# Rebuilding the attention part of a fused cross-read and expert-router kernel

## The chip, the cores and the metric

The kernel runs on one core of one Trainium2 chip. The metric is the device time of one execution in microseconds (us). Engines are written as in the profile: PE is TensorE (PEld its weight loads), DVE is VectorE, ACT is ScalarE, POOL is GpSimd, and SP issues most of the transfers.

## The reference, cut to what matters

Two parts follow each other. The first part has 8 batches of 8 heads; each head has 512 rows `x` and 32 states, both 64 wide. The second part sends each of the 8 x 544 resulting rows of 512 features to one of 8 experts.

```python
# first part, per batch and head (B, H, S, Ns, D = 8, 8, 512, 32, 64)
a  = softmax(scale * x @ state.T)      # over the 32 states of a row
xread = a @ state
a2 = softmax(scale * state @ x.T)      # over the 512 rows of a state
sread = a2 @ x
rows = concatenate([xread, sread])     # (512 + 32) rows of a batch; heads side by side: 512 features
# second part (N, D, E, F = 4352, 512, 8, 1024)
logits = normalize(rows) @ normalize(expert_emb).T / tau
e = argmax(logits);  gate = softmax(logits)[e]
out = gate * (relu(rows @ w1[e]) @ w2[e])
```

Everything is computed in fp32. The scores `x @ state.T` and `state @ x.T` of the first part are the same numbers, transposed.

## The kernel before

The program has three stages: the **attention part**, a **seam** that sorts the rows into blocks of one expert, and the **second part**, a loop over 41 blocks of 128 rows. The change lies in the attention part alone; the two other stages have the same instructions before and after.

A **unit** is one batch and one group of 4 heads, so that there are 16 units; 4 heads with 32 states each make 128 state rows, and 4 heads with 64 features make 256 columns. The states of a group stand as a block diagonal of 128 x 256 (`bdst`, with the 8 projections on the experts behind it, width 264).

- `states(b)`, once a batch: POOL copies the states into the block diagonal (L184), PE transposes it (`st_ps`, L190), ACT copies it out as `bd`, and PE projects it on the experts (`pj_ps`, L198).
- `scores(b, g)`: PE transposes the rows (`xt_ps`, L214, eight transposes), DVE and ACT copy a half each out as `xT`. PE then computes the scores twice: `sT_ps` with the states in partitions (L218) and `s_ps` with the rows in partitions (L223). The softmax over rows works on `sT_ps` and ends in `e2` and a diagonal matrix `dg` of the reciprocals of the sums (L238). The softmax over states works on `s_ps` and ends in `e1`, by the chain of a maximum (L245), a subtraction (L246), the exponential on ACT (L247), a sum (L248), a reciprocal (L250) and a multiplication on POOL (L251).
- `reads(b, g)`: PE transposes `e1` (`a_ps`, L258), turns `e2` by a matmul with `dg` that also scales it (`e_ps`, L263), and computes the two reads, `x_ps` (L270) and `sr_ps` (L278). The four `x_ps` banks are copied out by DVE and ACT in turns.
- `rows(b)` stores a batch's rows and chooses experts (`choose`); `state_rows(g)` does so for the state rows of 4 batches, after batches 3 and 7.

In the loop over units `scores` of unit u+1 is written ahead of `reads` of unit u, so it runs one unit ahead. A scheduler places each engine's instructions in one order that is fixed when the program is built; an engine then takes them strictly in that order, and a wait holds everything behind it. Most tiles of the loop (xn, xT, e1, e2 and others) have two buffers, PSUM has eight banks in rotation. A transfer takes one of eight semaphores in turn, and waits until the transfer that had it before has landed. `load_x` brings a batch's rows in four transfers, `load_w1` one expert's first weights.

Of the kernel before, what the change touches and what calls it, by code (L numbers as in the profile page):

```python
# [19 lines left out]
def kernel(  # L20
# [75 lines left out]
    with ExitStack() as att_ctx:  # L96
        att1 = att_ctx.enter_context(tc.tile_pool(name="att1", bufs=1))
        att = att_ctx.enter_context(tc.tile_pool(name="att", bufs=2))

# [10 lines left out]
        st_nat = att1.tile([P, B, HG, Dh], FP32, name="st_nat")  # L110
        nc.sync.dma_start(
            st_nat.rearrange("p b g d -> p (b g) d"),
            state.rearrange("b (g i) n d -> (i n) (b g) d", g=HG),
        )
# [458 lines left out]
```

## Time and profile before

| what | value |
|---|---|
| time, three runs | 885.47, 887.55 and 893.33 us (median 887.55) |
| the profiled execution, span from first to last instruction | 891.5 us (the profile lists no other time of it) |
| attention part, to the end of the last `sr_ps` matmuls | 0 to 209.1 us |
| seam, to the first transposes of a gathered block | 209.1 to 256.3 us |
| second part | 256.3 to 891.5 us |
| busy share of the span | PE 93%, PEld 52%, DVE 26%, ACT 16%, POOL 14% |

The span lies between the second and the third of the runs, 0.4% above the median. In the profile, "busy" of PE includes modelled ends of pipelined matmuls. Each fp32 matmul that is not a transpose shows as two instructions (two `sT_ps` matmuls as x4), a transpose as one. "PEclk" is the granted share of TensorE's full clock.

### The profile page before, as it was taken

The page shows a single profiled execution, that of the slowest core. Times are in us where ns is not written, and L with a number is a line of the kernel's source. Part 1 is how long each engine was busy: PE and PEld are TensorE (multiplying, and loading weights), DVE is VectorE, ACT ScalarE, POOL GpSimd, SP SyncE. Part 2 cuts the span into 40 slices and gives each one's busy share as a digit, 9 for nine tenths or more (in the row PEclk, how much of TensorE's full clock was granted, in tenths as well). Part 3 has the DMA queues.
Part 4 walks back from the last instruction along what each step waited for, and adds up shares of the span by engine and source line. Part 5 has one row for each costly group of instructions (what it writes and reads, how often), then busy time and mean ns, then how long its engine had stood idle before and what let it go on. Part 6 is the DMA issues. An engine that isn't in the chain of part 4 may idle for free.

```text
span 891.5 us, 8858 instructions
## 1 busy us (share of the span) xinstructions
PE 830.0 (93%) x3280; PEld 467.8 (52%) x3280; DVE 234.2 (26%) x514; ACT 138.5 (16%) x280; POOL 125.0 (14%) x192
## 2 busy tenths in 40 slices
PE   6899999995659999999999999999999999999995
PEld 4677777774624444454545454444444454545442
DVE  3454556546211112121212121211111121212110
ACT  3343444443001000000000010101000000000000
POOL 2111111110120111111111111111111111110000
PEclk9899999997569999999999999999999999999998
DMA  9486844311073454555545464636464545545340
GB/s 269 156 285 189 260 130 95 72 49 60 0 248 103 144 195 159 176 178 161 193 149 198 136 207 132 215 132 219 134 204 145 186 168 171 174 154 188 123 163 0
DMA packets 97553, 140.84 MB, mean 158 GB/s; under 512 B 38174, under 2 KB 46366, under 8 KB 97512
## 3 DMA queue, kind: packets, MB, share of 16 engines
q1 hardware_dynamic: 90920, 120.59, 41.9%
q0 software_dynamic: 6560, 19.67, 6.6%
q8 instruction: 27, 0.44, 0.2%
q14 instruction: 14, 0.11, 0.0%
q10 hardware_dynamic: 32, 0.02, 0.0%
HBM read 122.44 MB, written 19.66 MB: 159 GB/s over the span
## 4 chain that ended last, share of the span: by engine, by line
issue 62%; PE 20%; POOL 10%; DVE 5%; DMA 2%; POOLq 1%; ACT 1%; DVEq 0%
PE sT_ps L218 5%; POOL out_dram L517 4%; POOL xin L462 4%; PE s_ps L223 3%; PE x_ps L270 3%; PE sr_ps L278 3%; PE inv_ps L427 2%; PE e_ps L263 1%; DVE xT L70 1%; PE pj_ps L198 1%; DMA xin<-x_rows,src_row 1%; PE a_ps L258 1%; DMA x_rows<-xs 1%; PE xt_ps L214 1%; PE st_ps L190 1%
## 5 line engine op out<-in xcount | busy, mean ns | idle before, releaser
L512 PE MATMUL y_ps<-w,hT 128*128 128x512 f32 x656 | 292.4, 599 | 0.6 <-ACT hT L68 0.6
L486 PE MATMUL h_ps<-w_sb,xT 128*128 x656 | 289.4, 594 | 0.0
L486 PEld LDWEIGHTS h_ps<-w_sb,xT 128*128 128x128 f32 x656 | 125.1, 191 | 157.3 <-issue 157.2
L512 PEld LDWEIGHTS y_ps<-w,hT 128*128 128x128 f32 x656 | 121.3, 190 | 142.2 <-issue 137.3
L494 ACT ACTIVATE h<-h_ps 128x512 f32<-128x512 f32 x41 | 24.5, 597 | 467.6 <-PE h_ps L486 467.6
L516 DVE TENSOR_SCALAR y<-y_ps,gpos 128x512 f32<-128x512 f32 x41 | 30.8, 751 | 250.6 <-PE y_ps L512 250.6
L496 DVE TENSOR_SCALAR h<-h_ps 128x512 f32<-128x512 f32 x41 | 28.4, 692 | 254.4 <-PE h_ps L486 254.4
L517 POOL DMA_INDIRECT out_dram<-y,dst_row x41 | 41.6, 1015 | 307.5 <-DVE y L516 307.5
L462 POOL DMA_INDIRECT xin<-x_rows,src_row x41 | 42.2, 1030 | 261.0 <-PE xt_ps L475 237.8
L505 PEld LDWEIGHTS ht_ps<-ident,h 128*128 128x128 f32 x328 | 38.3, 140 | 21.6 <-issue 21.6
L218 PE MATMUL sT_ps<-xT,bd 128*128 128x512 f32 x64 | 40.9, 772 | 7.4 <-DVE xT L70 7.2
L68 ACT ACTIVATE hT<-ht_ps 128x512 f32<-128x512 f32 x41 | 24.5, 597 | 138.6 <-PE ht_ps L505 138.6
L505 PE MATMUL ht_ps<-ident,h 128*128 128x128 f32 x328 | 42.5, 272 | 0.0
L223 PEld LDWEIGHTS s_ps<-bd,xT 128*128 128x128 f32 x256 | 33.1, 200 | 11.1 <-issue 11.1
L475 PE MATMUL xt_ps<-ident,xin 128*128 128x128 f32 x164 | 25.6, 280 | 9.9 <-DMA xin<-x_rows,src_row 9.9
L270 PE MATMUL x_ps<-bdst,aT 128*128 128x264 f32 x128 | 33.4, 405 | 0.0
L278 PEld LDWEIGHTS sr_ps<-xn,a 128*32 128x32 f32 x512 | 29.0, 110 | 5.5 <-DVE r L248 4.5
L278 PE MATMUL sr_ps<-xn,a 128*32 128x64 f32 x512 | 31.6, 220 | 0.0
L223 PE MATMUL s_ps<-bd,xT 128*128 128x64 f32 x256 | 31.4, 277 | 0.0
L477 DVE COPY xT<-xt_ps 128x512 f32<-128x512 f32 x41 | 27.9, 681 | 10.6 <-PE xt_ps L475 10.6
L70 DVE COPY hT<-ht_ps 128x512 f32<-128x512 f32 x41 | 28.4, 692 | 7.6 <-PE ht_ps L505 6.9
L427 PE MATMUL inv_ps<-rr,oh 128*128 128x82 f32 x68 | 14.8, 422 | 15.5 <-POOL rr L420 15.5
(127 smaller groups left out, 469.4 us busy)
## 6 DMA issues: line engine op xcount, KB each, us to landing
w<-in_moe_w_dram SPq DMA_DIRECT2D x41, 2048.0 KB, 10.1
w_sb<-in_moe_w_dram SPq DMA_DIRECT2D x8, 2048.0 KB, 9.7
xn<-in_x_dram SPq DMA_DIRECT2D x32, 256.0 KB, 4.8
x_rows<-xr SPq DMA_DIRECT2D x16, 512.0 KB, 4.4
xin<-x_rows,src_row POOLq DMA_INDIRECT x41, 3.7
out_dram<-y,dst_row POOLq DMA_INDIRECT x41, 7.8
st_nat<-in_state_dram SPq DMA_DIRECT2D x1, 512.0 KB, 4.7
x_rows<-xs SPq DMA_DIRECT2D x2, 256.0 KB
```

The costliest lines, as they stand in the source:

```text
L70: eng.tensor_copy(dst, src)
L218: nc.tensor.matmul(sT, lhsT=bd[:, g, j], rhs=xT[:, j], start=(j == 0), stop=(j == 1))
L223: nc.tensor.matmul(s[:, c * P + j * half : c * P + j * half + half], lhsT=xT[:, j, c * P : c * P + P], rhs=bd[:, g, j, j * half : j * half ...
L270: nc.tensor.matmul(ps[:, 0:XW], lhsT=aT[:, c * P : c * P + P], rhs=bs[:, g], start=True, stop=True)
L278: nc.tensor.matmul(ps[q0 : q0 + Ns, i * Dh : i * Dh + Dh], lhsT=a2[:, c * P + i * Ns : c * P + i * Ns + Ns], rhs=xn[:, c, (HPG * g + i) * ...
L427: nc.tensor.matmul(inv_ps[:, 0 : 2 * NBLK], lhsT=oh[:, s], rhs=rr[:, s].rearrange("p t k -> p (t k)"), start=(s == 0), stop=(s == NSLOT - 1),)
L462: nc.gpsimd.indirect_dma_start(out=t, out_offset=None, in_=x_rows[:], in_offset=bass.IndirectOffsetOnAxis(ap=src_row[:, j : j + 1], axis=0 ...
L486: nc.tensor.matmul(ps, lhsT=xT[:, k * P : k * P + P], rhs=w1f[:, ds(ek * (KD * F) + k * F + i * 512, 512)], start=(k == 0), stop=(k == KD ...
L505: nc.tensor.transpose(ps[:, k * P : k * P + P], h[:, f0 : f0 + P], ident)
L512: nc.tensor.matmul(ps, lhsT=hT[:, k * P : k * P + P], rhs=w2[:, k], start=(k == 0), stop=(k == KF - 1))
L516: nc.vector.tensor_scalar(y, ps, gpos[:, j : j + 1], None, ALU.mult)
L517: ins = nc.gpsimd.indirect_dma_start(out=out[:], out_offset=bass.IndirectOffsetOnAxis(ap=dst_row[:, j : j + 1], axis=0), in_=y, in_offset= ...
```

## The change

The attention part gets a new shape.

- **Scores once.** Only `sT_ps` is computed, each pair of heads as a matmul of its own with 64 state columns, into a half of the partitions (L281 of the changed kernel). `s_ps` is gone. `e1` is now made by DVE's transpose of 32 x 32 squares from `sT_ps` (L295); the subtraction moves from DVE to POOL (L298); after the multiplication on POOL (L306) a second DVE transpose makes `aT` directly (L308). `a_ps` and its copy are gone.
- **State weights scaled, then transposed.** ACT multiplies `e2` by the reciprocal sums (L302); `e_ps` is now four transposes (L315) and no matmul with `dg`. ACT copies `e_ps` out (L317), and all four `x_ps` banks (L323); DVE no longer does.
- **States prepared once.** All transposed states (`bd`) and projections (`proj`) are made before the first unit, from two copies of the states in other layouts that come by ten transfers on ACT's queue, ahead of `emb` and `tau`. `states(b)` is then four transfers of 256-byte pieces into the block diagonal and a POOL copy of 8 columns a group.
- **Two units ahead.** `turn` of unit u+2 stands ahead of `reads(u)`, `scores` of u+2 behind it. `xT` halves, `aT` and `e2` have three buffers. The batches' rows come three batches ahead; every third batch lies in the place of the last expert's `w1`, whose load waits for that.

The core of the diff (comments that were removed are left out):

```diff
...
+        spare = w1_sb[:, E - 1].rearrange("p k f -> p (k f)")
         def load_x(b):
-            t = att.tile([P, NCH, D], FP32, tag="xn", name="xn")
+            if b % 3 == 2:
+                t = spare[:, 0 : NCH * D].rearrange("p (c d) -> p c d", c=NCH)
+            else:
+                t = att.tile([P, NCH, D], FP32, tag="xn", name="xn")
...
+        for b in range(B):
+            p0 = Ns * (b % 4)
+            nc.scalar.dma_start(st_row[p0 : p0 + Ns, b // 4], state[b].rearrange("h n d -> n h d"))
+        st_nat = [att.tile([P, B, Dh], FP32, tag="e2", name="st_nat", bufs=3) for _ in range(HG)]
+        for g in range(HG):
+            nc.scalar.dma_start(
+                st_nat[g], state[:, HPG * g : HPG * g + HPG].rearrange("b i n d -> (i n) b d")
+            )
...
         def states(b):
             bs = bdst[b % 2]
             for i in range(HPG):
-                nc.gpsimd.tensor_copy(
-                    bs[Ns * i : Ns * i + Ns, :, Dh * i : Dh * i + Dh], st_nat[Ns * i : Ns * i + Ns, b]
-                )
...
+                nc.sync.dma_start(
+                    bs[Ns * i : Ns * i + Ns, :, Dh * i : Dh * i + Dh],
+                    state[b].rearrange("(g i) n d -> i n g d", g=HG)[i],
+                )
+            nc.gpsimd.tensor_copy(bs[:, :, GW:XW], proj[:, b])
+            return bs
...
             sT = bank("sT_ps")
             for j in range(2):
-                nc.tensor.matmul(sT, lhsT=bd[:, g, j], rhs=xT[:, j], start=(j == 0), stop=(j == 1))
-            s = bank("s_ps")
...
+                o = j * 2 * Ns
+                nc.tensor.matmul(
+                    sT[o : o + 2 * Ns], lhsT=bd[b // 4][:, b % 4, 2 * g + j], rhs=xT[j], start=True, stop=True
+                )
...
+            nc.vector.transpose(e1f, sT)
             nc.scalar.activation(e2, sT, AF.Exp, bias=r2[:, 0:1], scale=SCALE, accum_out=r2[:, 1:2])
+            nc.vector.tensor_reduce(r1[:, 0].unsqueeze(2), e1, axis=AX, op=ALU.max)
+            nc.gpsimd.tensor_tensor(e1, e1, bc(r1[:, 0], shp, 2), ALU.subtract)
+            nc.scalar.activation(e1, e1, AF.Exp, scale=SCALE)
...
+            nc.scalar.activation(e2, e2, AF.Copy, scale=r2[:, 2:3])
...
             nc.gpsimd.tensor_tensor(e1, e1, bc(r1[:, 1], shp, 2), ALU.mult)
+            aT = att.tile([P, S], FP32, tag="aT", name="aT", bufs=3)
+            nc.vector.transpose(aT, e1f)
+            return aT, e2
...
             for c in range(NCH):
-                nc.tensor.matmul(
-                    ps[:, c * P : c * P + P], lhsT=e2[:, c * P : c * P + P], rhs=dg, start=True, stop=True
-                )
+                nc.tensor.transpose(ps[:, c * P : c * P + P], e2[:, c * P : c * P + P], ident)
...
-            if u + 1 < len(units):
-                b1, g1 = units[u + 1]
-                ready[u + 1] = scores(b1, g1, x_nat[b1], st[b1][1])
-            reads(b, g, x_nat[b], st[b][0], xr[b], *ready.pop(u))
+            later = u + 2 < len(units)
+            if later:
+                b2, g2 = units[u + 2]
+                xT = turn(b2, g2, x_nat[b2])
+            reads(b, g, x_nat[b], st[b], xr[b], *ready.pop(u))
+            if later:
+                ready[u + 2] = scores(b2, g2, xT)
```

The order of PE in one unit of the steady part, before (unit 1: the rows up to `s_ps` are unit 2's scores, with batch 1's states ahead of them):

```order
L190 MATMUL st_ps<-ident,bdst_107 128x128 x4
L198 MATMUL pj_ps<-enT,bd 128x8 x4
L214 MATMUL xt_ps<-ident,xn 128x128 x8
L218 MATMUL sT_ps<-xT,bd 128x512 x2
L223 MATMUL s_ps<-bd,xT 128x64 x8
L258 MATMUL a_ps<-ident,e_249 128x128 x4
L263 MATMUL e_ps<-dg,e_240 128x128 x4
L270 MATMUL x_ps<-bdst_106,aT 128x264 x4
L278 MATMUL sr_ps<-xn,a_373 32x64 x16
```

And in the changed kernel (unit 4; `sT_ps` at the end is unit 6's):

```order
L272 MATMUL xt_ps<-ident,xn 128x128 x8
L315 MATMUL e_ps<-ident,e_547 128x128 x4
L320 MATMUL x_ps<-bdst_121,aT 128x264 x4
L328 MATMUL sr_ps<-w_sb,a_690 32x64 x16
L281 MATMUL sT_ps<-xT,w_sb 64x512 x2
```

`st_ps`, `pj_ps`, `s_ps` and `a_ps` have left the loop, and `sT_ps` of the unit after next stands last.

The order of PE ahead of the first unit's reads in the changed kernel (`en_ps` are the experts, L151 and L159; `sb_ps` and `pj_ps` make the projections; two units' scores follow):

```order
L151 MATMUL en_ps<-ident,begin 128x8 x4
L159 MATMUL en_ps<-ident,begin 128x8 x8
L217 MATMUL st_ps<-ident,begin 128x128 x8
L234 MATMUL sb_ps<-ident,st_nat 128x128 x8
L242 MATMUL pj_ps<-begin 128x64 x8
L272 MATMUL xt_ps<-ident,xn 128x128 x8
L281 MATMUL sT_ps<-xT,w_sb 64x512 x2
L272 MATMUL xt_ps<-ident,xn 128x128 x8
L281 MATMUL sT_ps<-xT,w_sb 64x512 x2
L272 MATMUL xt_ps<-ident,xn 128x128 x8
L315 MATMUL e_ps<-ident,e_249 128x128 x4
L320 MATMUL x_ps<-bdst_121,aT 128x264 x4
```

Before, `en_ps` x4, `st_ps` x4 and `pj_ps` x4 stood ahead of the first `xt_ps`; now 12, 16 and 8 such steps do, and all of them stand behind the experts' row, the first on PE.

The order of DVE before in one unit (here `r2_343`, `r1_352` and `e1_353` belong to unit 2, `a2_373` to unit 1):

```order
L233 TENSOR_REDUCE r2_343<-sT_ps_331 128x1
L234 TENSOR_SCALAR r2_343<-r2_343 128x1
L245 TENSOR_REDUCE r1_352<-s_ps_334 128x16
L236 TENSOR_SCALAR r2_343<-r2_343 128x1
L246 TENSOR_TENSOR e1_353<-s_ps_334,r1_352 128x512
L237 RECIPROCAL r2_343<-r2_343 128x1
L267 COPY a2_373<-e_ps_368 128x512
L238 TENSOR_SCALAR dg_345<-ident_61,r2_343 128x128
L248 TENSOR_REDUCE r1_352<-e1_353 128x16
```

And in the changed kernel, around unit 6 (`r2_799`, `e1_804` and `sT_ps_796` belong to unit 7; `e1_730`, `r1_729` and `aT_743` to unit 6):

```order
L287 TENSOR_REDUCE r2_799<-sT_ps_796 128x1
L303 TENSOR_REDUCE r1_729<-e1_730 128x16
L288 TENSOR_SCALAR r2_799<-r2_799 128x1
L295 STREAM_TRANSPOSE e1_804<-sT_ps_796 128x512
L304 TENSOR_SCALAR r1_729<-r1_729 128x16
L344 TENSOR_TENSOR lg_70<-xr_670 128x32
L297 TENSOR_REDUCE r1_803<-e1_804 128x16
L305 RECIPROCAL r1_729<-r1_729 128x16
L201 TENSOR_REDUCE lmax_71<-lg_70 128x4
L70 COPY xT_849<-xt_ps_851 128x512
```

Before, a unit's own chain stands together up to its sum. Now unit 6's last transpose, `aT_743` (L308), stands three rows further on, and unit 7's maximum, the first of these rows, stands ahead of unit 6's sum (L303), reciprocal (L305) and last transpose, so those wait until `sT_ps` of unit 7 is there.

## Rows read from the trace of the kernel before

**Rows 1.** The page: its first line

```profile
span 891.5 us, 8858 instructions
```

**Rows 2.** Stretches: us, busy (instructions) of PE, PEld, DVE, ACT, POOL, clock, DMA share, GB/s

```profile
24.84:209.06 184.22, 171.13 (x1321) 136.46 (x1321) 95.72 (x277) 75.67 (x177) 28.60 (x68) 0.94 0.49 148
256.33:891.50 635.17, 624.92 (x1804) 303.15 (x1804) 112.19 (x164) 48.98 (x82) 80.58 (x79) 0.99 0.49 163
```

**Rows 3.** Timeline of PE over one unit and the next states: start, us, operation [idle before]

```profile
45.82 1.09 PE L214 MATMUL xt_ps<-ident,xn 128*128 128x128 f32 x8
47.54 1.98 PE L218 MATMUL sT_ps<-xT,bd 128*128 128x512 f32 x4 [0.62 <-DVE xT L70]
49.36 1.89 PE L223 MATMUL s_ps<-bd,xT 128*128 128x64 f32 x16
51.09 0.61 PE L258 MATMUL a_ps<-ident,e 128*128 128x128 f32 x4
51.54 1.06 PE L263 MATMUL e_ps<-dg,e 128*128 128x128 f32 x8
52.43 2.00 PE L270 MATMUL x_ps<-bdst,aT 128*128 128x264 f32 x8
54.37 1.97 PE L278 MATMUL sr_ps<-xn,a 128*32 128x64 f32 x32
56.27 0.66 PE L190 MATMUL st_ps<-ident,bdst 128*128 128x128 f32 x4
...
58.53 1.07 PE L214 MATMUL xt_ps<-ident,xn 128*128 128x128 f32 x8
```

**Rows 4.** Groups of instructions from 40 to 210 us: shapes, count | busy us, mean ns

```profile
L297 ACT ACTIVATE junk<-xr 128x512 f32<-128x512 f32 x32 | 20.1, 627 | 0.6
...
L251 POOL TENSOR_TENSOR e<-e,r 128x512 f32<-128x512 f32 x14 | 14.7, 1048 | 60.5 <-DVE r L250 60.0
...
L68 ACT ACTIVATE xr<-x_ps 128x264 f32<-128x264 f32 x30 | 11.7, 390 | 9.5 <-PE x_ps L270 8.1
...
L235 ACT ACTIVATE e<-sT_ps,r 128x512 f32<-128x512 f32 x14 | 9.6, 688 | 40.6 <-DVE r L234 40.6
...
L260 ACT ACTIVATE aT<-a_ps 128x512 f32<-128x512 f32 x15 | 9.0, 598 | 10.6 <-PE a_ps L258 10.6
...
L70 DVE COPY xT<-xt_ps 128x512 f32<-128x512 f32 x13 | 8.9, 688 | 3.0 <-PE xt_ps L214 2.9
...
L250 DVE RECIPROCAL r<-r 128x16 f32<-128x16 f32 x14 | 3.4, 242 | 0.0
...
L237 DVE RECIPROCAL r<-r 128x1 f32<-128x1 f32 x14 | 2.1, 153 | 0.0
```

**Rows 5.** Timeline of PE: one of the five slow `sT_ps` groups

```profile
83.31 3.58 PE L218 MATMUL sT_ps<-xT,bd 128*128 128x512 f32 x4 [0.68 <-DVE xT L70]
```

**Rows 6.** Stretches, columns as in rows 2: the start, and one slow `sT_ps` group

```profile
2.00:14.00 12.00, 6.84 (x26) 5.30 (x27) 2.69 (x11) 5.42 (x8) 4.62 (x28) 1.00 1.26 223
84.00:88.00 4.00, 4.00 (x15) 2.33 (x14) 0.84 (x2) 0.16 (x1) 0.00 (x0) 0.63 0.72 291
```

**Rows 7.** Timeline of the start, of PE and of ACT's transfer queue

```profile
0.76 0.62 ACTq L117 DMA_DIRECT2D emb<-in_moe_expert_emb_dram  x1
...
3.02 0.63 ACT L130 ACTIVATE junk<-emb 8x512 f32<-8x512 f32 x1
...
6.33 0.56 PE L138 MATMUL en_ps<-ident,emb 8*128 8x8 f32 x4 [6.33 <-POOL bdst L184]
6.82 1.15 PE L190 MATMUL st_ps<-ident,bdst 128*128 128x128 f32 x4
...
12.48 3.36 PE L218 MATMUL sT_ps<-xT,bd 128*128 128x512 f32 x4
...
26.86 2.98 PE L270 MATMUL x_ps<-bdst,aT 128*128 128x264 f32 x8
```

**Rows 8.** Timeline of PE: `state_rows` in the middle of the attention part

```profile
118.50 1.06 PE L314 MATMUL lg_ps<-enT,xsT 128*128 128x8 f32 x8 [0.95 <-DVE xsT L311]
```

More of the change, by code (lines that the diff above doesn't have):

```diff
@@ L108, in load_w1 @@
             nc.sync.dma_start(w1_sb[:, e], moe_w1[e].rearrange("(k p) f -> p k f", p=P))
[L110 to L113, printed above, removed]
-        )
+        begin = [att.tile([P, NCH * HG * XW], FP32, tag="xr", name="begin") for _ in range(2)]
+        st_row = begin[0][:, 0 : 2 * D].rearrange("p (q h d) -> p q h d", q=B // 4, h=H)
+        for b in range(B):
[6 more added lines that the diff above has]
+            )
         x_nat = {0: load_x(0)}
-        emb = att1.tile([P, D], FP32, tag="xsT", name="emb")[0:E]
+        emb = begin[1][0:E, 2 * D : 3 * D]
         nc.scalar.dma_start(emb, moe_expert_emb[:])
@@ L178, in choose @@
                 nc.gpsimd.tensor_tensor(cumx[:, s + 1], cumx[:, s], eq[:, s], ALU.add)
+        nbd = 4 * (H // 2) * 2 * Ns
+        bd = [spare[:, NCH * D : NCH * D + nbd], att1.tile([P, nbd], FP32, name="bd")]
+        bd = [t.rearrange("p (b j n) -> p b j n", b=4, j=H // 2) for t in bd]
+        for q in range(B // 4):
+            nc.vector.memset(bd[q], 0.0)
+            ps = bank("st_ps")
+            for j in range(H // 2):
+                nc.tensor.transpose(
+                    ps[:, j * P : j * P + P],
+                    st_row[:, q, 2 * j : 2 * j + 2].rearrange("p h d -> p (h d)"), ident,
+                )
+            src = ps.rearrange("p (j b n) -> p b j n", b=4, n=Ns)
+            for o in range(2):
+                copy(
+                    (nc.vector, nc.scalar)[o],
+                    bd[q][o * Dh : o * Dh + Dh, :, :, o * Ns : o * Ns + Ns],
+                    src[o * Dh : o * Dh + Dh],
+                )
+        sTb = begin[0][:, 2 * D : 4 * D].rearrange("p (g q n) -> p g q n", g=HG, q=B // 2)
+        for g in range(HG):
+            ps = bank("sb_ps")
+            for q in range(B // 2):
+                nc.tensor.transpose(
+                    ps[:, q * P : q * P + P], st_nat[g][:, 2 * q : 2 * q + 2].rearrange("p b d -> p (b d)"), ident
+                )
+            copy((nc.vector, nc.scalar)[g], sTb[:, g].rearrange("p q n -> p (q n)"), ps)
+        proj = att1.tile([P, B, HG, E], FP32, name="proj")
+        pp = bank("pj_ps").rearrange("p (g q c) -> p g q c", g=HG, q=B // 2)
+        for g in range(HG):
+            for q in range(B // 2):
+                nc.tensor.matmul(
+                    pp[:, g, q], lhsT=sTb[:, g, q], rhs=enb[:, g].rearrange("p b i e -> p (b i e)"),
+                    start=True, stop=True,
+                )
+        for i in range(HPG):
+            for g in range(HG):
+                copy(
+                    (nc.vector, nc.scalar)[g],
+                    proj[Ns * i : Ns * i + Ns, :, g].rearrange("p (q b) e -> p q b e", b=2),
+                    pp[Ns * i : Ns * i + Ns, g].rearrange("p q (b i e) -> p q b i e", b=2, e=E)[:, :, :, i],
+                )
         def states(b):
@@ L221, in scores @@
[L221 to L228 removed]
+                o = j * 2 * Ns
+                nc.tensor.matmul(
+                    sT[o : o + 2 * Ns], lhsT=bd[b // 4][:, b % 4, 2 * g + j], rhs=xT[j], start=True, stop=True
+                )
```

96 lines of the change are left out of this document (37 added, 59 removed).

## The prediction, on record before the changed kernel was timed

> **What bounds the kernel now.** I read the page first, for the span [rows 1], then the stretches [rows 2], then PE's timeline over one unit [rows 3]. The second part, 635.2 us with PE busy for 98% of it, has the same instructions afterwards, and so has the seam; I let both stand. What can move is the attention part, which ends at 209.1 us. From the first unit's reads on, at 24.84 us, PE is busy for 171.1 of 184.2 us (93%), while DVE has 95.7, ACT 75.7 and POOL 28.6 us [rows 2]. In the timeline one group of matmuls follows the other, and the one idle place in the unit shown is 0.62 us ahead of `sT_ps` [rows 3]. So PE's own work bounds this stage; the other engines have slack, but a change that takes work from PE soon meets their chains.
>
> [...]
>
> **PE's work in a unit.** Start to start in the timeline, a unit has `xt_ps` 1.1 (without its wait), `sT_ps` 1.82, `s_ps` 1.73, `a_ps` 0.45, `e_ps` 0.89, `x_ps` 1.94 and `sr_ps` 1.90 us; half of the units have 2.26 us for states besides [rows 3]. The change takes away `s_ps` (1.73), `a_ps` (0.45), half of `e_ps` (four transposes, like `a_ps`: 0.45 for 0.89) and the states (1.13 a unit). What is left is 1.1 + 0.45 + 1.94 + 1.90 + 1.82 = 7.2 us, for 11.0 plus the waits: some 60 us over 16 units, if nothing else took PE's place.
>
> **The other engines' work in a unit.** ACT, by the mean durations [rows 4]: `xT` and `e_ps` copies 2 x 0.6, two exponentials of 0.69 and, like a square, 0.63, some 0.2 for reading out a sum, the new scaling about 0.69 (a row operand like the first exponential's), four `xr` 1.56, and half of a batch's four squares 1.6: 6.5 us. DVE: six passes over 128 x 512 (two maxima, a sum, `xT`, two transposes) at 0.69 are 4.1; small ones, `xs` and choosing 1.9: 6.0. POOL: two at 1.05 and trifles, 2.5. None exceeds 7.2, so none is the bound by its sum.
>
> **An unknown price** is DVE's transpose, which the trace of before does not have. From below I bound it by the copy of 264 columns on ACT, 0.39, about half the width; from above by 3.2, from the reciprocals, DVE's slowest per element: (242 - 153) / 15 = 5.9 ns, times 512, plus 0.15 [rows 4]. I take 0.69, the copy of the same shape out of PSUM. [...]
>
> **The chain that is left.** From the end of `sT_ps` to `aT` a unit passes DVE 0.69, DVE 0.69, DVE 0.69, POOL 1.05, ACT 0.63, DVE 0.69 and about 0.4 of small ones, POOL 1.05, DVE 0.69: 6.6 us, about 7 with hand-overs. With two units ahead it has 7.2 + 1.55 us. It fits, where DVE's fixed order lets it. I walked through that order unit by unit with these prices:
> - In 11 units the whole chain stands ahead of the next unit's maximum: no wait, 7.2 us.
> - In three (3, 8, 11) the reciprocal stands behind it. Then `aT` comes only after maximum, transpose and reciprocal (1.7), POOL (1.05) and the transpose (0.75), 3.55 us after `sT_ps`, where PE wants it after 1.55: 2.05 us each, 6.2.
> - In units 6 and 14 (the rows shown for unit 6) even the sum stands behind it, and POOL subtracts for the next unit first: `aT` comes after 5.9 us: 4.4, and 5.5 at the end of the part.
> - In the middle, PE's `state_rows` stands ahead of the next rows' transposes, and its copy `xsT` on DVE stands behind unit 9's whole chain; PE waited 0.95 us there [rows 8] and now waits some 6. With its own matmuls 7.5 us.
>
> PE's work is 16 x 7.2 = 115.2, less 1.55 (counted from the first `x_ps`) and 5.84 (the last two units turn and score nothing): 107.8. With 6.2 + 4.4 + 5.5 + 7.5 and 0.5 for small waits, 131.9 us from the first `x_ps` to the last `sr_ps`.
>
> **Clock drops.** Each slow group cost about 1.5 us (1.6 in the one shown, 3.58 less 1.98 [rows 3, 5]). I expect seven, after the five long waits, the middle and the start: 10.5. [...]
>
> **The start.** Before, `emb` is the first transfer on ACT's queue, read at 3.02 us, and `en_ps` could run at 6.33 [rows 7]; the first `x_ps` came at 26.86. Now ten state transfers, 1 MB, stand ahead of `emb` and `tau`, in three rounds of waits for semaphores, beside SP's rows. From 2 to 14 us the queues moved 223 GB/s, their share over 1 [rows 6]; if the two queues share that, `emb` lands when 2 MB are through: 2 + 9.4 us and a round trip, about 13 (between 9 and 16). Then 3.3 us for the experts' chain (3.02 to 6.33), two copies and a second turn, some 2.5; 16 transposes at the start's 0.29 [rows 7], copies, `pj_ps`, together 9; `xt_ps` and copies 2.7, `sT_ps` 2 to 3.4: the first scores end near 32.5. Two units' chains interleave on DVE from there, with the exponential's table load: `aT` after 9.5. First `x_ps` at **42 us** (36 to 46), 15 later than before.
>
> **What costs nothing.** SP's 32 new transfers for block diagonals lie in a queue that mostly waits for results; each is needed a batch later. Rows come three batches ahead, so some 15 us of slack cover them; without it a 1 MB load would show with about 5 us. The last expert's `w1` is loaded some 14 us ahead of the part's end, and 2 MB at the start's 223 GB/s take 9.4 [rows 6]; beyond that it would delay the last stored rows, and so the seam, by a few us.
>
> **Sum.** 42 + 131.9 + 10.5 = 184.4 for 209.1: 24.7 us less, of a span of 891.5 [rows 1]. That span is 4 above the median of the runs, so I take the difference from the median: 887.55 - 24.7 = **863 us**. About 1%, 9 us, is what a measurement of this kernel can tell from no change.
>
> **Rivals.**
> - *PE's halves overlap, or the waits vanish.* The two `sT_ps` matmuls use different columns of the array. If they run at once, 0.9 us a unit leaves the path in some 12 units, and if DVE's order costs half of what I walked, 10 more: 841 to 853. For it: nothing else uses the columns. Against: the trace has only matmuls of one column place in a row (32 `sr_ps` in 1.97 us). [...] 25%.
> - *The clock falls in nearly every unit.* Shorter units with waits after 1.55 us of transposes: nine more drops, 14 us, or drops that last twice as long, 20: 877 to 885, about no change. For it: drops follow waits. Against: `pj_ps` and the 0.69 wait behind `st_ps`, which stood ahead of the drops, leave the loop. 15%.
> - *DVE becomes the bound, and the kernel slower.* It has 6.0 us a unit with two transposes at 0.69. At 2 us DVE has 8.6, and each late `aT` is later by two transposes; the units then take about 10.5, and with 15 us lost at the start nothing is gained. That is the point from which it decides; at 3.2 DVE has 11.0 and a unit takes 12.5: 42 + 200 + 682 = 924 us of span, 920. For it: the operation isn't in the trace. Against: DVE's pass of this width out of PSUM takes 0.69 [rows 4]. 9%.
> - *The start costs much more,* `emb` after all rows: x_ps at 50, 871; inside the range.
>
> My case has 51%. The range is **840 to 883**: below it lies the first rival's far end, above it the third and the end of the second. Faster by over 1%: 0.78, within 1% 0.12, slower 0.10.
>
> **What would show it.** First `x_ps` near 42 us. PE's groups in a quiet unit start to start as above, 7.2 us, and `x_ps` of units 3, 6, 8 and 11 waiting for DVE's `aT`. STREAM_TRANSPOSE at 0.6 to 0.8 us. `sT_ps` at 1.8 us: under 1.4, its halves overlap. PE's clock from the first `x_ps` on at 0.90 to 0.95; under 0.85, the second rival. The second part at 635 us. I am wrong if ACT, at 6.5 of 7.2 us a unit, is what PE waits for, or if the span from the first to the last `x_ps` is not near 140.

## The result, and the profile of the changed kernel

| | before | changed |
|---|---|---|
| time, median (lowest to highest), 4 runs each | 889.78 us (885.47 to 893.33) | 862.38 us (860.98 to 863.83) |
| profiled execution: span | 891.5 us | 859.2 us |
| first `x_ps` | 26.9 us | 41.3 us |
| first `x_ps` to the end of the last `sr_ps` | 182.2 us | 134.8 us |
| seam | 47.3 us | 47.4 us |
| second part | 635.2 us | 635.8 us |

The ratio of the times is 0.968 (95% interval 0.964 to 0.972). The spans differ by 32.3 us, the medians by 27.4, because the profiled execution of before (893.33 us) was its longest and that of the changed kernel (860.98 us) its shortest.

The page's first line and four stretches of the changed kernel, with the columns of [rows 2]: the loop from the first `x_ps` on, the second part, a quiet unit, and the surroundings of unit 6's `x_ps`:

```profile
span 859.2 us, 8026 instructions
```

```profile
41.27:176.03 134.76, 110.75 (x873) 82.91 (x874) 78.97 (x219) 83.77 (x211) 36.73 (x64) 0.88 0.61 181
223.43:859.20 635.77, 625.22 (x1804) 303.26 (x1804) 112.19 (x164) 48.95 (x82) 80.36 (x79) 0.99 0.49 163
66.00:71.00 5.00, 5.00 (x47) 3.56 (x47) 2.65 (x8) 4.80 (x13) 1.19 (x2) 1.00 0.01 1
86.00:93.00 7.00, 3.03 (x7) 2.42 (x8) 4.80 (x18) 5.40 (x14) 3.65 (x6) 0.66 0.82 238
```

PE was busy for 93% of its loop before [rows 2]; now it is for 110.8 of 134.8 us, 82%, at a granted clock of 0.88. PE no longer bounds this stage alone. The timeline of PE over one quiet unit answers to [rows 3]:

```profile
49.01 1.10 PE L272 MATMUL xt_ps<-ident,xn 128*128 128x128 f32 x8
49.95 0.60 PE L315 MATMUL e_ps<-ident,e 128*128 128x128 f32 x4
50.38 1.95 PE L320 MATMUL x_ps<-bdst,aT 128*128 128x264 f32 x8
52.26 1.97 PE L328 MATMUL sr_ps<-xn,a 128*32 128x64 f32 x32
54.16 1.08 PE L281 MATMUL sT_ps<-xT,w_sb 128*64 128x512 f32 x4
55.17 1.09 PE L272 MATMUL xt_ps<-ident,w_sb 128*128 128x128 f32 x8
```

Start to start, a unit takes 55.17 - 49.01 = 6.16 us, where 7.2 were forecast: `sT_ps` takes 1.01 us, not 1.82. Other places of the same timeline: the first `x_ps`, that of unit 3, unit 6 with the longest wait ahead of an `x_ps` but one, and the middle, which answers to [rows 8]:

```profile
41.27 3.89 PE L320 MATMUL x_ps<-bdst,aT 128*128 128x264 f32 x8 [2.24 <-DVE r L304]
...
65.75 2.02 PE L320 MATMUL x_ps<-bdst,aT 128*128 128x264 f32 x8 [2.45 <-DVE r L300]
...
89.97 3.89 PE L320 MATMUL x_ps<-bdst,aT 128*128 128x264 f32 x8 [4.33 <-DVE r L301]
...
112.14 1.88 PE L364 MATMUL lg_ps<-enT,xsT 128*128 128x8 f32 x8 [8.04 <-DVE xsT L361]
113.87 1.95 PE L272 MATMUL xt_ps<-ident,w_sb 128*128 128x128 f32 x8
```

Behind most of the long waits a group takes about twice its usual time (`x_ps` 3.89 for 1.95, `xt_ps` 1.95 for 1.09), but not behind all: unit 3's `x_ps` took 2.02 behind 2.45 us, unit 0's 3.89 behind 2.24. From 86 to 93 us the granted clock is 0.66, over unit 6's `x_ps` alone (89.97 to 93.79) 0.50, over unit 3's (65.75 to 67.70) and in the quiet unit 1.00. Before, the slow groups were `sT_ps` [rows 5]; now they are the `x_ps` of units 0, 6, 8, 11 and 14.

Why unit 6 waits stands in DVE's and POOL's timelines. First DVE, then POOL:

```profile
83.21 0.42 DVE L334 COPY xs<-sr_ps 32x256 f32<-32x256 f32 x1 [1.80 <-PE sr_ps L328]
84.26 0.69 DVE L287 TENSOR_REDUCE r<-sT_ps 128x1 f32<-128x512 f32 x1 [0.62 <-PE sT_ps L281]
84.87 0.68 DVE L303 TENSOR_REDUCE r<-e 128x16 f32<-128x512 f32 x1
...
86.89 0.24 DVE L305 RECIPROCAL r<-r 128x16 f32<-128x16 f32 x1
...
89.20 0.71 DVE L308 STREAM_TRANSPOSE aT<-e 128x512 f32<-128x512 f32 x1 [0.99 <-POOL e L306]
```

```profile
87.12 1.05 POOL L298 TENSOR_TENSOR e<-e,r 128x512 f32<-128x512 f32 x1 [4.58 <-DVE r L297]
88.12 1.05 POOL L306 TENSOR_TENSOR e<-e,r 128x512 f32<-128x512 f32 x1
```

Unit 6's sum (L303) could start when ACT's exponential (L299, 82.57 and 0.63 long) ended, at 83.20. It stands behind unit 7's maximum (L287), which waits for `sT_ps`; its reciprocal (L305) stands behind unit 7's transpose, and its multiplication on POOL behind unit 7's subtraction. `aT` is there at 89.9, and `x_ps` starts at 89.97.

### The profile page after: what moved, and what is told of

It reads as the page before. It is cut to its first block, busy times and chain, and to the rows that moved or that the text cites. A ratio compares the mean times of both kernels' runs of the same rounds, so it can differ in the third digit from the quotient of the medians.

```text
span 859.2 us, 8026 instructions
## 1 busy us (share of the span) xinstructions
PE 767.7 (89%) x2840; PEld 413.1 (48%) x2840; DVE 224.3 (26%) x472; ACT 151.2 (18%) x327; POOL 132.7 (15%) x184
## 4 chain that ended last, share of the span: by engine, by line
issue 64%; PE 13%; POOL 11%; DVE 6%; DMA 4%; ACT 1%; POOLq 1%; ACTq 0%; DVEq 0%
POOL out_dram L570 5%; POOL xin L515 5%; PE x_ps L320 4%; PE sr_ps L328 3%; PE inv_ps L480 2%; PE sT_ps L281 1%; DMA begin<-in_state_dram 1%; DMA xin<-x_rows,src_row 1%; DMA begin<-in_moe_expert_emb_dram 1%; PE xt_ps L272 1%; POOL e L306 1%; DVE r L287 1%; DMA x_rows<-xs 1%; DVE r L303 1%; DVE e L295 1%
## 5 line engine op out<-in xcount | busy, mean ns | idle before, releaser
L320 PE MATMUL x_ps<-bdst,aT 128*128 128x264 f32 x128 | 40.2, 468 | 17.5 <-DVE r L300 4.9
L68 ACT ACTIVATE hT<-ht_ps 128x512 f32<-128x512 f32 x41 | 24.5, 597 | 139.1 <-PE ht_ps L558 132.0
L320 PEld LDWEIGHTS x_ps<-bdst,aT 128*128 128x128 f32 x128 | 28.1, 231 | 24.6 <-issue 5.7
L530 DVE COPY xT<-xt_ps 128x512 f32<-128x512 f32 x41 | 27.9, 681 | 10.7 <-PE xt_ps L528 10.3
L328 PEld LDWEIGHTS sr_ps<-xn,a 128*32 128x32 f32 x384 | 23.6, 116 | 5.1 <-ACT xr L323 2.0
L328 PE MATMUL sr_ps<-xn,a 128*32 128x64 f32 x384 | 25.6, 229 | 0.0
L298 POOL TENSOR_TENSOR e<-e,r 128x512 f32<-128x512 f32 x16 | 16.8, 1047 | 56.5 <-DVE r L300 25.0
L528 PEld LDWEIGHTS xt_ps<-ident,xin 128*128 128x128 f32 x164 | 19.7, 144 | 10.6 <-issue 10.2
```

Source lines behind the costliest of these rows:

```text
L320: nc.tensor.matmul(ps[:, 0:XW], lhsT=aT[:, c * P : c * P + P], rhs=bs[:, g], start=True, stop=True)
L328: nc.tensor.matmul(ps[q0 : q0 + Ns, i * Dh : i * Dh + Dh], lhsT=a2[:, c * P + i * Ns : c * P + i * Ns + Ns], rhs=xn[:, c, (HPG * g + i) * ...
L528: nc.tensor.transpose(ps[:, k * P : k * P + P], t[:, k * P : k * P + P], ident)
```

## Experiments

Twelve kernels ran; ratios are to the kernel before, which ran beside each (its medians there were 888.2 to 891.5 us). "Loop" is always the time from the first `x_ps` to the end of the last `sr_ps` in the profiled execution.

### Which part of the change brings how much

**Scores once, alone.** The kernel before, with `s_ps`, `a_ps` and their copies gone and DVE's squares in their place; one unit ahead as before.

```diff
-  s = bank("s_ps")
...
-  nc.vector.tensor_reduce(r1[:, 0].unsqueeze(2), s3, axis=AX, op=ALU.max)
-  nc.vector.tensor_tensor(e1, s3, bc(r1[:, 0], shp, 2), ALU.subtract)
+  nc.vector.transpose(e1f, sT)
+  nc.vector.tensor_reduce(r1[:, 0].unsqueeze(2), e1, axis=AX, op=ALU.max)
+  nc.gpsimd.tensor_tensor(e1, e1, bc(r1[:, 0], shp, 2), ALU.subtract)
...
-  ps = bank("a_ps")
...
-  nc.scalar.activation(aT, ps, AF.Copy)
+  nc.vector.transpose(aT, e1f)
```

> Edit: the kernel before with one part of the change alone: scores computed once, turned in 32 x 32 squares on DVE, subtraction on POOL, aT by the second turn; s_ps and a_ps gone; states, dg and one unit ahead as before; xT in three half buffers for space. Theory (PE's own work is the bound, and this is the largest part of it): 1.73 + 0.45 us a unit leave PE, 35 us over 16 units, some given back to waits for the chain (6.6 us against 9.7 of lead) and clock drops: 855 to 866 us, 0.960 to 0.973, as good as the whole change since the start stays as before. Rival (the chain through DVE and POOL is too slow one unit ahead): x_ps waits in most units, 880 us or more.

Measured: 882.39 us, ratio 0.992 (0.989 to 0.994). Its loop, with the columns of [rows 2]:

```profile
27.12:198.30 171.18, 140.44 (x1025) 105.29 (x1026) 103.64 (x288) 63.43 (x160) 42.65 (x82) 0.94 0.55 159
```

The loop takes 171.2 us for 182.2, and PE is busy for 140.4 of them. PE lost 2.2 us a unit [rows 3], 35 in all, and 11 came out. The theory failed.

**And the weights scaled, then transposed.** On top of that kernel:

```diff
-  nc.vector.tensor_scalar(dg, ident, r2[:, 2:3], None, ALU.mult)
+  nc.scalar.activation(e2, e2, AF.Copy, scale=r2[:, 2:3])
...
-  nc.tensor.matmul(ps[:, c * P : c * P + P], lhsT=e2[:, c * P : c * P + P], rhs=dg, start=True, stop=True)
+  nc.tensor.transpose(ps[:, c * P : c * P + P], e2[:, c * P : c * P + P], ident)
```

> The kernel before with scores once (882.4 us), and now the state weights scaled on ACT and transposed, without the diagonal matrix: e_ps is four transposes for eight instructions. PE has 0.45 us a unit less, 7 us in all, DVE 0.15 a unit less, ACT 0.7 more. Theory (with one unit ahead PE waits for chains anyway, only part of PE's saving comes out, as 10 of 35 us did with scores once): 878 to 882. Rival (PE's time comes out whole): 874 to 876. If it is the first, the rest of the change, states once and the order, is worth some 17 us.

Measured: 880.34 us, 0.990 (0.987 to 0.993), loop 170.2. Of 7 us of PE's time about 1 to 2 came out, which the two intervals do not tell from nothing. From 20 to 185 us, PE waited 14.6 us ahead of `sT_ps` and 14.6 ahead of `x_ps`; in the kernel with scores once alone it was 12.1 and 11.7.

**One unit ahead instead of two,** the other parts as in the change:

```diff
...
-  b2, g2 = units[u + 2]
-  xT = turn(b2, g2, x_nat[b2])
+  b1, g1 = units[u + 1]
+  ready[u + 1] = scores(b1, g1, turn(b1, g1, x_nat[b1]))
   reads(b, g, x_nat[b], st[b], xr[b], *ready.pop(u))
...
-  ready[u + 2] = scores(b2, g2, xT)
```

> Edit: the changed kernel with one unit ahead: turn and scores of u+1 both ahead of reads of u; buffers as changed. From the end of sT_ps to x_ps of its unit PE then has e_ps, x_ps, sr_ps, xt_ps, sT_ps, e_ps between, 6.8 us by the changed kernel's groups, against 7.5 two units ahead. Theory (the lead is about the same, the place in DVE's order decides): waits ahead of x_ps grow by at most 0.7 us a unit, 862 to 874 us, 0.968 to 0.982. Rival (two ahead is what makes the rebuilt chain fit, as the change's title has it): a wait in every unit of 3 us or more, 905 us and above.

Measured: 861.28 us, 0.968 (0.962 to 0.973), loop 137.2. "Two units ahead" as the change writes it brings nothing that shows. So the step from 880.34 to 861.28, 19 us, is that of the states made once, with what comes with it: `sT_ps` in halves, `e_ps` and `x_ps` copied out by ACT, buffers, rows that come three batches ahead. The two loops, first the one of 880.34 us:

```profile
28.53:198.71 170.18, 136.24 (x965) 96.91 (x966) 102.61 (x276) 70.60 (x174) 42.85 (x82) 0.93 0.53 149
43.66:180.83 137.17, 113.39 (x881) 81.09 (x882) 83.67 (x222) 86.11 (x215) 37.09 (x64) 0.94 0.62 181
```

The second is 33 us shorter, by 22.9 us of PE's busy time and 10.2 of its idle time, and starts 15 us later. Only the halves were tried apart:

**`sT_ps` with all 128 columns again** (zero blocks in `bd`, two matmuls accumulating; for space, `xT` has two buffers instead of three):

```diff
-  nc.tensor.matmul(sT[o : o + 2 * Ns], lhsT=bd[b // 4][:, b % 4, 2 * g + j], rhs=xT[j], start=True, stop=True)
+  nc.tensor.matmul(sT, lhsT=bd[b // 4][:, b % 4, 2 * g + j], rhs=xT[j], start=(j == 0), stop=(j == 1))
```

> Edit: each pair of heads' scores with all 128 state columns, the other pair's columns zero, the two matmuls accumulated, as before the change; everything else as changed. Theory (the halves of sT_ps overlap on PE, which took 0.8 us a unit off the path beyond the forecast): sT_ps start to the next group goes from 1.0 to 1.8 us in every unit, 14 x 0.8 = 11 us more in the loop and 1.6 at the start, 872 to 876 us, ratio to before 0.980 to 0.985. Rival (the waits for DVE set the length, PE's own groups do not): the waits ahead of x_ps shrink by what sT_ps grows, 862 to 865 us, 0.968 to 0.972.

Measured: 864.99 us, 0.972 (0.968 to 0.976). `sT_ps` takes 1.82 us again, 0.81 more in 13 of the loop's 14 (in unit 14 of the change the halves stand apart and gain nothing), which is 10.5 us of PE; the loop is 139.1 us, 4.3 longer, and the time 2.6. The rival's range holds it. Its loop:

```profile
41.19:180.31 139.12, 116.57 (x873) 87.70 (x874) 81.15 (x222) 85.55 (x215) 36.99 (x65) 0.91 0.60 176
```

Of the other 6.2 us only 1.5 come off the waits (22.5 us idle for 24.0). PE's busy time grows by 5.8 us and not by 10.5, at a clock of 0.91 for 0.88: its slow groups cost 9.2 us more than their usual time, for 12.6 in the change.

### Where the waits come from

**DVE's order, pinned:** a unit's maximum behind the last transpose (`aT`) of the unit before, in DVE's row and without a semaphore.

```diff
...
-  nc.vector.tensor_reduce(r2[:, 0:1], sT, axis=AX, op=ALU.max)
+  top = nc.vector.tensor_reduce(r2[:, 0:1], sT, axis=AX, op=ALU.max)
+  if last_aT:
+      behind(top, last_aT[-1])
...
-  nc.vector.transpose(aT, e1f)
+  last_aT.append(nc.vector.transpose(aT, e1f))
```

> Edit: a unit's maximum (first DVE step of its chain) is queued behind the unit before's last transpose aT; nothing else. Theory (DVE's fixed order makes the late aT of units 3, 6, 11 and 14): these four waits of 2.45, 4.33, 2.44 and 4.77 us and the slow x_ps behind three of them (1.9 each) go, none above 1 us is left ahead of x_ps in the loop; 10 to 18 us less than the change, 844 to 852 us, 0.949 to 0.958. Rival (the chain itself is too long or ACT holds it, whatever the order): the waits spread over other units, same sum, 860 to 866 us.

Measured: 877.93 us, 0.984 (0.978 to 0.990). The theory failed: slower by 15 us than the change. The timeline of PE, two units of it:

```profile
77.40 3.68 PE L331 MATMUL x_ps<-bdst,aT 128*128 128x264 f32 x8 [2.35 <-DVE aT L319]
...
87.66 3.67 PE L331 MATMUL x_ps<-bdst,aT 128*128 128x264 f32 x8 [2.21 <-DVE aT L319]
```

In 11 of 16 units `x_ps` now waits 1.5 to 2.7 us for `aT`, most of them then take 2.9 to 3.7 us, and the unit between the two rows takes 10.3 (87.66 - 77.40). DVE's timeline in the same place:

```profile
86.89 0.71 DVE L319 STREAM_TRANSPOSE aT<-e 128x512 f32<-128x512 f32 x1 [1.22 <-POOL e L317]
87.53 0.65 DVE L296 TENSOR_REDUCE r<-sT_ps 128x1 f32<-128x512 f32 x1
...
97.30 0.70 DVE L319 STREAM_TRANSPOSE aT<-e 128x512 f32<-128x512 f32 x1
```

The pin takes away the late sums, and with them the overlap of two units' chains: the next chain starts only where the one before ends, and the one shown takes 10.5 us (87.53 to 98.00). DVE's mixing of units was what hid a chain longer than a unit.

**The experts' transfer first on ACT's queue** (`emb`, `tau` ahead of the ten state transfers):

```diff
...
+  nc.scalar.dma_start(emb, moe_expert_emb[:])
...
+  nc.scalar.dma_start(tau, moe_tau.to_broadcast([E, 1]))
...
   nc.scalar.dma_start(st_row[p0 : p0 + Ns, b // 4], state[b].rearrange("h n d -> n h d"))
...
-  nc.scalar.dma_start(emb, moe_expert_emb[:])
...
-  nc.scalar.dma_start(tau, moe_tau.to_broadcast([E, 1]))
```

> Edit: emb and tau are the first transfers on ACT's queue, the states behind them. Theory (PE's start waits for emb behind 1 MB of states): en_ps goes from 21.9 us to 7 or so, st_ps waits for the states at 10 to 12, sb_ps and pj_ps for the second copy at 14 to 17; first x_ps at 33 to 37 instead of 41.3, 5 to 8 us less, 854 to 857 us, 0.960 to 0.964. Rival (the transfers as a whole bind the start): the second copy of the states, now last, lands at 18 as emb did, first x_ps at 39 to 41, no change.

Measured: 853.69 us, 0.960 (0.956 to 0.964). The first `x_ps` comes at 36.14 us, 5.1 earlier, and the loop is 131.3, 3.5 shorter. So some 5 of the 8.7 us are the start. The rest is mostly PE's busy time, 107.7 us for 110.8, with fewer slow groups (the granted clock over the loop is 0.90 for 0.88); PE's idle time is 23.6 us for 24.0, and the middle's wait has grown to 9.1. The start itself varies: in the next kernel, whose edit lies far behind it, the first `x_ps` came at 43.5 us, 2.2 later than in the change.

**Batch 3's rows and state rows ahead of the next scores,** for the middle's wait:

```diff
   reads(b, g, x_nat[b], st[b], xr[b], *ready.pop(u))
+  early = g == HG - 1 and b % GB == GB - 1 and later
+  if early:
+      rows(b, xr.pop(b))
+      state_rows(b // GB)
...
   ready[u + 2] = scores(b2, g2, xT)
...
```

> Edit: after batch 3 its rows and state rows are written ahead of the next scores instead of behind them. Theory (lg_ps waits 8.0 us because xsT stands behind unit 9's chain on DVE, and PE cools): that wait falls to about 1 us and the slow lg_ps, xt_ps and e_ps behind it go; 7 to 10 us less, 852 to 855 us, 0.958 to 0.962. Rival (unit 8's aT and e_ps would wait anyway): the wait moves to x_ps of unit 8 or 9, 859 to 863 us.

Measured: 859.29 us, 0.966 (0.962 to 0.970). The rival: the middle's wait falls from 8.04 to 3.51 us, and unit 11's, some units on, grows from 2.44 to 3.47; loop 131.9. In the change `lg_ps` and `xt_ps` behind the 8.04 us ran at a granted clock of 0.50 (112.14 to 115.60), 1.88 and 1.95 us long; here `lg_ps` still takes 1.88 behind the 3.51.

**All three edits together** (pin, experts first, rows ahead):

> Edit: the changed kernel with the three edits together: DVE's order (maximum behind the unit before's aT), emb and tau first on ACT's queue, batch 3's state rows ahead of the next scores. Theory: the three add, 14 + 6 + 8 us at the centres, 830 to 842 us, 0.933 to 0.946. Rival (ACT, 84 of 135 us busy in the loop of the changed kernel, is the next bound): waits for ACT appear ahead of e_ps, x_ps and sr_ps and eat half of it, 845 to 850 us.

Measured: 862.22 us, 0.971 (0.965 to 0.978), loop 143.0. The theory failed, and not by its rival: waits for DVE's `aT` stand ahead of `x_ps`, 20.9 us in the loop, as with the pin alone. The two other edits did bring something, 15.7 us against the pinned kernel; what the pin costs took it up again. And the last two without the pin:

> The changed kernel with two of the edits at once: the experts' transfer first on ACT's queue, and the fourth batch's rows and state rows written ahead of the next scores. If the two gains are independent (one is at the start, one in the middle), the sum of their single gains: 862.4 - 8.7 - 3.1, about 850.5. Rival: the middle's wait returns as a wait for aT in the following units, as it partly did when the edit stood alone (first to last sr_ps 131.9 us against 134.8): 851 to 854, not to be told from the experts' edit alone (853.7).

Measured: 849.04 us, 0.956 (0.951 to 0.960). That fits gains of start and middle that add up, 862.4 - 8.7 - 3.1 = 850.6.

### How much room a chain has

These runs left one reading. A unit's chain, from the end of `sT_ps` to `aT`, takes at best 7.7 us in the changed kernel: unit 2's `sT_ps` ends at 49.08 and its `aT` (DVE's timeline, first row and last) at 56.8.

```profile
49.13 0.69 DVE L287 TENSOR_REDUCE r<-sT_ps 128x1 f32<-128x512 f32 x1 [0.61 <-PE sT_ps L281]
...
56.11 0.70 DVE L308 STREAM_TRANSPOSE aT<-e 128x512 f32<-128x512 f32 x1
```

Unit 6's takes 12.9 (77.0 to 89.9). But PE's order has `sT_ps` of unit u+2 *behind* the reads of unit u. From its end to `x_ps` of unit u+2 there are one turn and one `e_ps` (1.35 us together) and one more unit: 7.5 us, less than the shortest chain. One unit ahead gives not much less (six groups of a unit lie between, some 6.6 us without waits), which fits that run's showing no difference. The test is to give a chain more room with the same instructions in another order:

```diff
...
+  turned = turn(*units[2], x_nat[units[2][0]])
...
-  xT = turn(b2, g2, x_nat[b2])
+  ready[u + 2] = scores(*units[u + 2], turned)
...
+  turned = turn(b3, g3, x_nat[b3])
   reads(b, g, x_nat[b], st[b], xr[b], *ready.pop(u))
...
-  ready[u + 2] = scores(b2, g2, xT)
```

Here `turned` is the turn of a unit made one step earlier, and `xT` has four buffers for three. Two units and 1.35 us, 13.7 us, then lie between.

It ran first on the kernel with the experts first:

> On the kernel with the experts' transfer first (853.7 us): the turn runs three units ahead and sT_ps of unit u+2 is written ahead of the reads of unit u, so that PE's row has sT_ps ahead of e_ps and x_ps, no longer behind sr_ps. Theory (the slack is what is short): until now sT_ps of a unit ended about 8.4 us ahead of its x_ps, and the chain over DVE, POOL and ACT takes 7.6 at best and up to 12.8; now it has some 14, so the waits of x_ps for aT vanish, and with them the x_ps at half the clock; first x_ps to last sr_ps from 131.3 down to 112 to 118, bounded by ACT (6.5 us a unit), time 834 to 842. Rival (the in-order work of DVE and ACT is itself the bound, 83 and 85 us of 135 spread badly): the waits only change their place, 850 to 858. Another rival: the middle wait for xsT grows, because more of a chain stands ahead of it: 845 to 850.

Measured: 839.93 us, 0.942 (0.936 to 0.947), loop 114.7. (One of its four executions took 3087 us. It is in the median, and not in the ratio; the other three took 835.73, 838.90 and 840.96 us. The next kernel, with the same loop, had none like it.) Then alone, on the changed kernel:

> The changed kernel (862.4 us) with the one edit that the turn runs three units ahead and scores of unit u+2 are written ahead of the reads of unit u; the experts' transfer stays where the change has it. Theory (short slack is what the change's loop lost by; independent of the start): as much less as on the kernel with the experts first, 13 to 15: 847 to 850, first x_ps to last sr_ps near 115 us for 134.8. Rival (the gain needs the earlier start, because transfers of rows and weights then become the bound): 852 to 860.

Measured: 841.40 us (839.45 to 841.88), 0.946 (0.943 to 0.949): 21 us less than the change, where 13 to 15 were expected. The loop's stretch, and a unit in PE's timeline:

```profile
43.05:153.77 110.72, 99.35 (x863) 75.68 (x862) 76.40 (x215) 82.70 (x212) 36.28 (x64) 0.94 0.73 211
```

```profile
46.83 1.08 PE L281 MATMUL sT_ps<-xT,w_sb 128*64 128x512 f32 x4
47.84 1.09 PE L272 MATMUL xt_ps<-ident,w_sb 128*128 128x128 f32 x8
48.77 0.60 PE L315 MATMUL e_ps<-ident,e 128*128 128x128 f32 x4
49.21 1.95 PE L320 MATMUL x_ps<-bdst,aT 128*128 128x264 f32 x8
51.09 1.97 PE L328 MATMUL sr_ps<-xn,a 128*32 128x64 f32 x32
52.99 1.08 PE L281 MATMUL sT_ps<-xT,w_sb 128*64 128x512 f32 x4
```

A unit still takes 6.16 us, but no `x_ps` waits for `aT` any more, and none is slow (where its eight instructions stand together they take 1.95 us); PE's busy time falls from 110.8 to 99.4 us, most of it by that, and its idle time from 24.0 to 11.4. DVE and ACT do the same work as before (76.4 for 79.0, 82.7 for 83.8 us), so neither was the bound: the room was.

The scheduler also ordered DVE anew: in the units looked at (2 to 6), a unit's sum now stands ahead of the next unit's maximum. If that had made the chains short enough for the old room, the room would not be the cause. It did not. Unit 4's chain, in DVE's timeline, and its `x_ps` in PE's:

```profile
54.89 0.67 DVE L287 TENSOR_REDUCE r<-sT_ps 128x1 f32<-128x512 f32 x1
...
64.14 0.71 DVE L308 STREAM_TRANSPOSE aT<-e 128x512 f32<-128x512 f32 x1 [0.62 <-POOL e L306]
```

```profile
70.44 1.95 PE L320 MATMUL x_ps<-bdst,aT 128*128 128x264 f32 x8
```

Its `sT_ps` ended at 54.07 us, so that the chain takes 10.8 us, and `aT` is there 5.6 us ahead of `x_ps`. From unit 2 on the chains take 7.6 to 12.1 us, 9.3 in the mean (7.7 to 12.9 and 9.5 in the change): none would have fitted into 7.5 us, and each `aT` is now there some 1.5 us or more ahead of its `x_ps`. The waits that are left in the loop are the middle's (4.64 us), one of 1.1 for a copy on DVE, and five for ACT, of 0.3 to 1.9 us.

With the experts first as well (the run before this one) the first `x_ps` came at 40.9 us for 43.1, but the loop was 4 us longer (114.7), and the time is the same within the intervals; why the earlier start is worth nothing there is open.

**The middle, once more.** On the kernel with room and the experts first, `lg_ps` is written one unit later than the transposes `xst_ps`, and `xsT` has a buffer of its own (`state_logits` is the part of `state_rows` from `lg_ps` on):

```diff
...
   reads(b, g, x_nat[b], st[b], xr[b], *ready.pop(u))
+  if late is not None:
+      state_logits(*late)
+      late = None
...
-  state_rows(b // GB)
+  late = state_rows(b // GB)
...
```

> On the kernel with scores ahead of the reads and the experts first (839.9 us): the state rows' logits (lg_ps) are written a unit later than their transposes and the copy xsT, which gets its own buffer; xT has three buffers for four. Theory (the middle wait of 4.3 us for xsT holds PE up only because lg_ps stands in PE's row right behind the transposes): the wait goes, and with it the groups at half the clock behind it (sT_ps 1.98 for 1.08, xt_ps 1.97 for 1.09), together 6 us: 832 to 835. Rival (the wait stands for work that DVE is late with anyway and comes back ahead of the next x_ps, or three buffers are short): 838 to 842.

Measured: 831.70 us (830.82 to 833.74), 0.935 (0.932 to 0.939), the best version, 31 us below the change. The loop's stretch, and PE in the middle:

```profile
38.44:145.56 107.12, 94.92 (x863) 72.38 (x862) 75.76 (x220) 83.18 (x212) 36.88 (x64) 1.00 0.76 223
```

```profile
92.08 0.76 PE L359 MATMUL xst_ps<-ident,xs 128*128 128x128 f32 x4
93.41 1.08 PE L281 MATMUL sT_ps<-xT,bd 128*64 128x512 f32 x4 [0.57 <-DVE xT L70]
...
99.56 1.06 PE L371 MATMUL lg_ps<-enT,xsT 128*128 128x8 f32 x8
```

The theory held: nothing waits at the middle's `lg_ps`, and the granted clock rounds to 1.00 over the whole loop. The loop is 7.5 us shorter than in the kernel that it builds on, where 6 were expected; that kernel's profiled execution also began its loop 2.5 us later (40.9 for 38.4), with the same steps of PE ahead of it, some of which took longer (`sT_ps` 2.72 for 1.79, `xt_ps` 1.97 for 1.09), so that part of the gain in time may be chance.

## Why the prediction was right, and where it was not

The time forecast, 863 us, hit the median to 1 us, but that is better than its working, and in part luck. By the sum, the profiled span should have been 42 + 142.4 + 682.4 = 866.8 us; it was 859.2, 7.6 less. Of that, 4.9 us are that the two profiled executions lie on opposite sides of their medians (32.3 us apart, the medians 27.4), and 2.2 that the difference was taken from the first median of before, 887.55, and not from 889.78. So 24.7 us were forecast and 27.4 measured, and the lower starting point made up for most of that.

- **Start: right, by another split, so by chance.** 41.27 us for 42. ACT's square of `emb` started at 18.56 us, not near 13; what followed took 22.7 us instead of 29.
- **PE's work in a unit: wrong, above all by one term, `sT_ps`.** A quiet unit takes 6.16 us for 7.2: `sT_ps` has 0.81 of that, and `xt_ps` 0.17 (0.93 for 1.1, which had been read ahead of a wait). PE's busy time in the loop is 98.2 us without the slow groups' excess (110.75 - 12.6), where the sum had 109.3 (107.8 and the middle's 1.5): 11.1 less, of which `sT_ps` has 13 x 0.81 = 10.5 (in unit 14 its halves stand apart). This was the first rival's mechanism; its price, 841 to 853, needed the waits to vanish too, and they did not.
- **The waits: right in place and sum, by chance in part.** Named were units 3, 6, 8, 11, 14 and the middle, 22.1 us (with 6 of the middle's 7.5); measured are 2.45, 4.33, 0, 2.44, 4.77 and 8.04, together 22.0. The middle's wait was 2 us longer, and unit 8's `aT`, there at 107.2 us, lay long ahead of its `x_ps` behind it (116.5).
- **The clock: right in size.** Forecast 10.5 us for seven slow groups; measured 12.6, as the excess of `x_ps` of units 0, 6, 8, 11 and 14, of the groups next to them and of the middle's `lg_ps`. That `x_ps` is hit and not `sT_ps` was not said, and the granted clock was 0.88, under the 0.90 to 0.95 that it gave as a sign.
- **"PE's own work bounds this stage": the step that failed.** It added PE's work and the waits as if they were separate. The full-width `sT_ps` showed that of 10.5 us of PE only 4.3 come out, and the reordered kernel that the same instructions need 110.7 us, not 134.8. The chain's room was computed (7.2 + 1.55 for 7) and read as "it fits"; in the shorter unit it is 7.5 us, for chains of 7.7 to 12.9, and it was the bound. One of the prediction's own signs of being wrong came with it: from the first to the last `x_ps` it is 131 us, where near 140 was wanted.
- **No cost elsewhere: right.** Seam 47.4 us for 47.3 [rows 2], second part 635.8 for 635.2.
- **DVE's transpose: right.** 0.704 and 0.709 us for 0.69, out of PSUM and out of SBUF; ACT's new scaling 0.715 for 0.69. Rows of the loop's groups, with the columns of [rows 4]:

```profile
L308 DVE STREAM_TRANSPOSE aT<-e 128x512 f32<-128x512 f32 x16 | 11.3, 709 | 9.2 <-POOL e L306 9.1
L302 ACT ACTIVATE e<-e,r 128x512 f32<-128x512 f32 x14 | 10.0, 715 | 2.2 <-DVE r L301 2.0
L295 DVE STREAM_TRANSPOSE e<-sT_ps 128x512 f32<-128x512 f32 x14 | 9.9, 704 | 0.0
```

The third rival had its condition at 2 us and fell with that. The second needed a clock under 0.85: it was 0.88, and the pinned kernel shows the case itself, 0.84 over its loop and 878 us (by its own 20 us its far end is 883 us, not 885).

What is not settled: which of the parts that come with the states made once carries most of the 19 us (of `sT_ps` in halves it is known that going back costs 2.6 us in the change); and why an earlier start is worth 8.7 us in the change and nothing measurable in the kernel with more room.

## What to carry to other kernels

Where an engine's work in a stage is cut, compare the chain through the other engines with the room that the engine's *own order* leaves between producing and consuming, counted in the new, shorter unit; "two units ahead" in the code is one unit if the producer stands behind the consumer of an older unit. When the room is less than the chain, time taken from the engine comes back as waits, and some of the longer waits cost again by the clock (unit 6's `x_ps`, behind 4.33 us, took 3.89 for 1.95 at a granted 0.50); moving the producer ahead of the older reads was worth 21 us here with the same instructions in another order. Forcing the order of a helper engine can cost more than the waits that it takes away: here the pin ended the overlap of two chains, and the kernel was 15 us slower.

## What the runs showed of the hardware

- **Two matmuls into different halves of the partitions ran at once,** 1.01 us for both where one alone took 1.00. For unit 14 the halves stand apart in PE's timeline:

```profile
150.81 1.07 PE L281 MATMUL sT_ps<-xT,bd 128*64 128x512 f32 x2
151.81 0.77 PE L272 MATMUL xt_ps<-ident,xn 128*128 128x128 f32 x5
152.50 1.07 PE L281 MATMUL sT_ps<-xT,bd 128*64 128x512 f32 x2
153.51 0.55 PE L272 MATMUL xt_ps<-ident,xn 128*128 128x128 f32 x3
```

One half alone holds PE for 1.00 us to the next start; both in a row take 1.01 in the quiet unit. No idle time shows where the width changes from 32 to 64 and to 128 columns (in that unit `sr_ps` ends at 54.23 and `sT_ps` starts at 54.16, ends at 55.24, and `xt_ps` starts at 55.17); why a half takes 1.00 us where one of the two full-width matmuls takes 0.91 (half of 1.82) is open.

- **The transfers that ACT issued held up its own work here.** On ACT the ten state transfers' issues last until 11.8 us, and a 16 KB transfer behind them landed at 18.5. With `emb` first the square still started only at 13.45, behind the last state transfer's issue, which ended at 12.1, and a table load of 1.28. The rows of the change:

```profile
11.88 2.00 ACTq L129 DMA_DIRECT2D begin<-in_moe_expert_emb_dram  x1
...
18.56 0.63 ACT L143 ACTIVATE junk<-begin 8x512 f32<-8x512 f32 x1 [3.01 <-DMA begin<-in_moe_expert_emb_dram]
```

- **The granted clock fell behind long waits, but not behind all of them.** It was 0.50 over unit 6's `x_ps`, behind 4.33 us. Over the loop it was granted at 0.84 with waits of 1.5 to 2.7 us in 11 of 16 units (the pin), 0.88 in the change, 0.94 where no `x_ps` waits for `aT`, and 1.00 where the middle's wait is gone too, the longest left being 2.6 us. PE's idle time in the last two loops is nearly the same, 11.4 and 12.2 us, so its sum does not decide; and of two waits of 2.4 us in the change one (unit 11) was followed by an `x_ps` of 3.61 us, at a clock of 0.54 (139.16 to 142.70), the other (unit 3) by one of 2.02, at 1.00. Even the same steps of PE at the start ran at different speeds in two kernels (`xt_ps` 1.97 us and 1.09). What decides is not shown.
